# Gated linear attention and a rational MLP on one core: alpha loaded first, k turned in 112 columns, last products by token block, and GpSimd waits for VectorE operations on its port

## The chip, the cores and the metric

The kernel runs on one core of a Trainium2 chip. A core has five engines that work side by side, each through its own list of instructions in the order in which they were issued: TensorE (PE, matrix products), VectorE (DVE), ScalarE (ACT), GpSimd (POOL) and SyncE (SP, which here only issues transfers, or DMAs). An instruction waits on semaphores until what it needs is done, and what stands behind it on its engine waits too. The metric is the device time of one execution in microseconds (us), less is better. All times below are in us unless marked ns.

## The reference

Two stages. The first is gated linear attention over q, k, v, alpha of shape (4, 8, 768, 48): batch, head, token, width.

```
for t in range(S):
    state = alpha[:, :, t, :, None] * state + einsum('bhd,bhe->bhde', k[:, :, t], v[:, :, t])
    y[:, :, t] = einsum('bhd,bhde->bhe', q[:, :, t], state)
```

y becomes x, 3072 tokens by 384. The second stage is an MLP with 2048 hidden units and a rational activation:

```
h = x @ w_in
g = (a0 + a1*h + a2*h**2 + a3*h**3) / (1 + |b0|*|h| + |b1|*h**2 + 1e-6)
out = g @ w_out
```

w_in and w_out arrive as float64, everything else as float32.

## The kernel before

Attention is cut into 24 chunks g of 128 tokens, six for each batch, with the eight heads as four pairs side by side. For a chunk VectorE forms the running products of alpha from behind (L445) and from the front (L457), k and q are multiplied by them (L472, L475, on POOL or DVE), PE makes the scores (L489), ACT copies them out (L496), POOL masks them (L500), PE turns k (L507) for the state's update and ACT copies it out (L510), the state is decayed (L513), and PE makes the chunk's output (L531, once with the state, once with scores and v) and the update (L550), which DVE adds (L560). The first four chunks' inputs come in whole lines (L393) and are turned on PE (L410); the others come as 32-row pieces (L386) and are turned on DVE (L437, L442).

The weights arrive as 64-bit words (L240, L243) in sixteen pieces, each joined into float32 (ACT L252 and L264, DVE L260 and L280) and split into a high and a low part (ACT L295; DVE or POOL L300), so that three products of reduced width stand for one exact one. The MLP's blocks u = 0 to 9 use whole float32 words (L625, L638); the others, u = 10 to 95, use the parts (L652 in; L671 out). Each block's 128x512 tile of h goes through a chain: ACT L698 (|h|) and L701, POOL or ACT L705/L707 (q1), POOL L710 (qm), DVE L721, L725, ACT L728, L731, DVE L735, L738, L744 (g), and for wide blocks ACT L747 (high part gh) and POOL or DVE L751 (low part gl). For the last 512 tokens PE puts tokens into rows (L665), and DVE and ACT copy the four token blocks out (L691, L689) and SP and ACT store them (L695).

What is computed is a list of some 2700 steps, each with an engine, some with an alternative engine, and what it comes after. The order in which steps are issued, and which take their alternative, stands in a packed table (ORDER) that `Plan.run` (L45) reads; each engine keeps that order. A step's costs and due times do not act when a table is read. A step has a mark `lock` where it is a VectorE operation that shares an SBUF port with GpSimd; before the change the mark has no effect on what is issued.

Of the kernel before, what the change touches and what calls it, by code (L numbers as in the profile page):

```python
# [24 lines left out]
class Plan:  # L25
# [42 lines left out]
    '0d~B7VXm8jc35aFbHh9~gKSq@$FwvPY;OC=OtiyoT{Fo}#mS-b>{Of8JTUX^NIS(AG1KfcJZ5I#J@b!kY{G0&^UO@Q6-',
    '~HpZ3f%vILgkjGx4TrV;0(n=82hUN89Hn#Iy=oU}xh?Gse!cdF)s_2i0^pvuzVo*(|YZ?JKj?j<c`LI$OznHH$(Q+bZU',
    'kd1IE@Z|1i7Vyc>cX1yJ1cG>0jt=Skl$Nn^p%nG}~el&S)Q?uKyv~z6-^Vw{&n{BB1WmegfHlOWbw%FCSr`c*x*>`4--',  # L70
    'DcmLxj4Y=3*B$On?Gi+-EI%qzh;Luu*NPzfPbx+8}^48Xb#%b_H5{Xw!fK&3-Gt;WFkN>bJHHOJMB4(aK;WYhwVcA$Fw',
    '!Q%@KRv&c{2Zk2z{D*kg7velXAN3wzt%vKMV+hy{Z~^4oj%l3juY>_~ImMga?#?R`sd#h$PXcWmE~t5%?$xn?_>0PfnC',
# [1067 lines left out]
```

## Time and profile before

| what | us |
|---|---|
| three runs | 548.06, 546.98, 545.26 (median 546.98) |
| profiled execution | 545.37, its span 543.6 |
| PE busy | 523.7 (96%) |
| DVE busy | 483.4 (89%) |
| ACT busy | 439.5 (81%) |
| POOL busy | 404.0 (74%) |

The span runs from the first to the last event of the profiled execution; 1.77 us of its own time lie around it. Busy shares are means over stages with different limits: attention and the preparation of weights fill DVE in the first fifth, and the wide blocks fill PE after it. A bracket such as [1.66 <-DVE t L744] at the end of a timeline row says that the engine had been idle for 1.66 us and that the operation of DVE at L744 that wrote t released it. A row with x12 stands for twelve instructions in a run. A mean duration of a product is longer than the pitch of a run of them, since they are pipelined.

### The profile page before, as it was taken

The page shows a single profiled execution, that of the slowest core. Times are in us where ns is not written, and L with a number is a line of the kernel's source. Part 1 is how long each engine was busy: PE and PEld are TensorE (multiplying, and loading weights), DVE is VectorE, ACT ScalarE, POOL GpSimd, SP SyncE. Part 2 cuts the span into 40 slices and gives each one's busy share as a digit, 9 for nine tenths or more (in the row PEclk, how much of TensorE's full clock was granted, in tenths as well). Part 3 has the DMA queues.
Part 4 walks back from the last instruction along what each step waited for, and adds up shares of the span by engine and source line. Part 5 has one row for each costly group of instructions (what it writes and reads, how often), then busy time and mean ns, then how long its engine had stood idle before and what let it go on. Part 6 is the DMA issues. An engine that isn't in the chain of part 4 may idle for free.

```text
span 543.6 us, 11871 instructions
## 1 busy us (share of the span) xinstructions
PE 523.7 (96%) x4350; PEld 433.0 (80%) x4350; DVE 483.4 (89%) x717; ACT 439.5 (81%) x737; POOL 404.0 (74%) x377
## 2 busy tenths in 40 slices
PE   8889898999999999999999999999999999999994
PEld 8778687788788777878788887888788877889994
DVE  2989989999998899999999999998899797888872
ACT  3899798999997788768787778898877778779781
POOL 2567677899997798788578667877788675786772
PEclk9998899999999999999999999999999999999998
DMA  9959966654543535643455232442553410040001
GB/s 251 307 117 279 247 170 156 143 127 117 134 126 81 129 77 116 118 118 66 102 111 108 60 74 58 94 97 69 112 114 72 93 23 20 2 78 1 1 1 61
DMA packets 146174, 57.46 MB, mean 106 GB/s; under 512 B 133056, under 2 KB 138688, under 8 KB 146112
## 3 DMA queue, kind: packets, MB, share of 16 engines
q1 hardware_dynamic: 145824, 56.27, 44.4%
q8 instruction: 35, 0.57, 0.5%
q10 hardware_dynamic: 288, 0.39, 0.2%
q14 instruction: 27, 0.22, 0.1%
HBM read 47.98 MB, written 4.72 MB: 97 GB/s over the span
## 4 chain that ended last, share of the span: by engine, by line
PE 66%; DVE 9%; DMA 9%; SPq 9%; issue 2%; ACT 2%; POOL 1%; DVEq 0%; ACTq 0%
PE ps L652 27%; PE ps L671 22%; PE ps L665 6%; SPq L386 5%; PE ps L531 4%; DMA wo_words<-in_moe_w_out_dram 4%; PE ps L489 3%; DMA wi_words<-in_moe_w_in_dram 3%; SPq L240 2%; PE ps L638 2%; DMA raw_a<-in_alpha_dram 1%; DVE t L725 1%; DVE ps L738 1%; DVE t L721 1%; DVE t L744 1%
## 5 line engine op out<-in xcount | busy, mean ns | idle before, releaser
L652 PE MATMUL ps<-x,wi 128*128 128x512 f32 x774 | 209.6, 397 | 0.2 <-DVE t L744 0.2
L671 PE MATMUL ps<-gh_gl,wo 128*128 128x512 f32 x630 | 176.0, 400 | 0.4 <-ACT gh_gl L747 0.4
L652 PEld LDWEIGHTS ps<-x,wi 128*128 128x128 f32 x774 | 143.7, 188 | 33.1 <-DVE t L744 1.7
L710 POOL TENSOR_TENSOR qm<-qm,ah 128x512 f32<-128x512 f32 x96 | 127.3, 1326 | 30.2 <-ACT qm L707 21.6
L671 PEld LDWEIGHTS ps<-gh_gl,wo 128*128 128x128 f32 x630 | 115.4, 188 | 27.9 <-ACT gh_gl L747 0.8
L751 POOL TENSOR_TENSOR gh_gl<-t,gh_gl 128x512 fp32r<-128x512 f32 x76 | 98.9, 1302 | 33.3 <-ACT gh_gl L747 11.3
L701 ACT ACTIVATE t<-ps,coef 128x512 f32<-128x512 f32 x96 | 74.3, 774 | 15.8 <-PE ps L652 9.2
L698 ACT ACTIVATE ah<-ps 128x512 f32<-128x512 f32 x96 | 57.2, 596 | 34.0 <-PE ps L652 24.5
L735 DVE SCALAR_TENSOR_TENSOR t<-t,coef,ps 128x512 f32<-128x512 f32 x96 | 70.7, 738 | 15.1 <-ACT ps L731 14.5
L721 DVE TENSOR_TENSOR t<-t,ps 128x512 f32<-128x512 f32 x96 | 64.9, 676 | 14.6 <-ACT t L701 10.7
L728 ACT ACTIVATE ps<-qm,one_eps 128x512 f32<-128x512 f32 x96 | 66.3, 691 | 11.7 <-POOL qm L710 5.9
L725 DVE SCALAR_TENSOR_TENSOR t<-t,coef,ps 128x512 f32<-128x512 f32 x96 | 70.9, 740 | 2.0 <-ACT ah L698 0.7
L705 POOL TENSOR_SCALAR qm<-ah,bab 128x512 f32<-128x512 f32 x53 | 43.0, 811 | 37.2 <-ACT ah L698 28.7
L744 DVE SCALAR_TENSOR_TENSOR t<-ps,t 128x512 f32<-128x512 f32 x96 | 65.8, 686 | 1.9
L738 DVE SCALAR_TENSOR_TENSOR ps<-qm,ps 128x512 f32<-128x512 f32 x96 | 66.0, 687 | 0.0
L747 ACT ACTIVATE gh_gl<-t 128x512 fp32r<-128x512 f32 x86 | 53.9, 627 | 7.0 <-DVE t L744 6.7
L731 ACT ACTIVATE ps<-ps 128x512 f32<-128x512 f32 x96 | 56.0, 584 | 1.8
L665 PE MATMUL ps<-wo,gh_gl 128*128 128x384 f32 x192 | 38.0, 339 | 0.0
L445 DVE TENSOR_TENSOR_SCAN tg<-ta,ps 128x528 f32<-128x528 f32 x24 | 29.9, 1244 | 8.7 <-ACT ta L429 8.7
L472 POOL TENSOR_TENSOR tqk<-tqk,tg 128x512 f32<-128x512 f32 x22 | 29.5, 1340 | 10.2 <-ACT parts L252 9.0
L665 PEld LDWEIGHTS ps<-wo,gh_gl 128*128 128x128 f32 x192 | 34.4, 188 | 2.4 <-ACT gh_gl L747 0.3
L500 POOL TENSOR_SCALAR_AFFINE_SELECT sc<-sc 128x1024 f32<-128x1024 f32 x24 | 26.9, 1120 | 12.0 <-ACT sc L496 9.7
(114 smaller groups left out, 745.3 us busy)
## 6 DMA issues: line engine op xcount, KB each, us to landing
raw_qk<-in_q_dram SPq DMA_DIRECT2D x160, 48.0 KB, 2.1
raw_a<-in_alpha_dram SPq DMA_DIRECT2D x160, 48.0 KB, 2.1
raw_qk<-in_k_dram SPq DMA_DIRECT2D x160, 48.0 KB, 2.1
wi_words<-in_moe_w_in_dram SPq DMA_DIRECT2D x8, 768.0 KB, 7.9
wo_words<-in_moe_w_out_dram SPq DMA_DIRECT2D x8, 768.0 KB, 7.0
tv<-in_v_dram SPq DMA_DIRECT2D x24, 192.0 KB, 3.2
wr<-in_alpha_dram SPq DMA_DIRECT2D x18, 256.0 KB, 3.0
out_dram<-parts SPq DMA_DIRECT2D x60, 64.0 KB, 2.1
```

What stands on the lines that cost most here:

```text
L652: nc.tensor.matmul(h_of(u), w(key)[:, kt * FU + f % FU, :], x[:, kt, xp, :], start=(n == 0), stop=(n == len(todo) - 1),)
L665: nc.tensor.matmul(bank(T_BANKS[tt], DM), g[:, tt * P : (tt + 1) * P], w(("o", f // FU))[:, f % FU, :], start=(f == 0 and first_w), stop=( ...
L671: nc.tensor.matmul(bank(O_BANKS[dt]), w(("o", f // FU))[:, f % FU, dt * P : (dt + 1) * P], g, start=(f == 0 and first_w), stop=(f == NF - ...
L701: nc.scalar.activation(buf(s, "t1", u), h_of(u), AF.Identity, bias=a2, scale=a3)
L710: nc.gpsimd.tensor_tensor(buf(s, "qm", u), buf(s, "qm", u), buf(s, "ah", u), op=ALU.mult)
L721: nc.vector.tensor_tensor(t, t, h_of(u), op=ALU.mult)
L725: nc.vector.scalar_tensor_tensor(t, t, a1, h_of(u), op0=ALU.add, op1=ALU.mult)
L728: nc.scalar.activation(h_of(u), buf(s, "qm", u), AF.Abs_reciprocal_sqrt, bias=one_eps)
L735: nc.vector.scalar_tensor_tensor(t, t, a0, h_of(u), op0=ALU.add, op1=ALU.mult)
L738: nc.vector.scalar_tensor_tensor(h_of(u), buf(s, "qm", u), 1.0 + 1e-6, h_of(u), op0=ALU.add, op1=ALU.mult)
L744: nc.vector.scalar_tensor_tensor(t, h_of(u), 2.0, t, op0=ALU.subtract, op1=ALU.mult, reverse0=True)
L751: eng.tensor_tensor(buf(s, "gl", u).rearrange("p a b -> p (a b)"), buf(s, "t1", u), gh, op=ALU.subtract)
```

## The change

Six edits. Numbers after L are lines of the kernel before. (1) The first three loads on SP's queue are alpha, k, q; before, q, alpha, k. (2) PE's first instructions, transposes of the identity that write to nothing used (L403), number 20; before, 28. ACT gets a first instruction "prime" on a 128x1 tile, and the memset of one_eps that it reads stands earlier on POOL. (3) k is turned in 112 columns: a pair of heads fills 64 + 48 rows, and the last 16 of 128 held nothing needed; the copy after it has 448 columns in place of 512, and 16 columns of the tile get zeros once. (4) The twelve products of the last block, u = 95, go by token block, through `last_out`. (5) For each VectorE step with the mark `lock`, the next POOL step in the issued order gets a wait for it; the step "tot" gets the mark when it is on DVE. (6) The table is new, as the steps' numbers are, but the order on each engine is otherwise kept; constants of the planner (SV, WIDE, kb and the like) change and are not read.

The diff, without the table's rows but the first of each and without numbers that only the planner reads:

```diff
@@ -42,102 +42,112 @@
-    def run(self, engines):
+    def run(self, engines, tc):
...
+        info = mybir.DependencyInfo(mybir.DependencyClass.Sync, mybir.DependencyReason.DATA)
+        held = None
         for n in order:
             key = keys[n & 0x7FFF]
             s = self.steps[key]
             assert all(a in done or a not in self.steps for a in s["after"])
+            mode = s["alt"] if key in self.other else s
+            old = len(tc.nc.cur_bb.bb.instructions)
             if s["alt"]:
-                s["fn"](engines[(s["alt"] if key in self.other else s)["eng"]], *s["args"])
+                s["fn"](engines[mode["eng"]], *s["args"])
             else:
                 s["fn"](*s["args"])
+            new = tc.nc.cur_bb.bb.instructions[old:]
+            if mode["lock"]:
+                held = new[-1]
+            elif mode["eng"] == "POOL" and held is not None:
+                tc.add_manual_dep(new[0], held.name, info, reason="shared port")
+                held = None
             done.add(key)
 
 
 ORDER = [
-    'c-jTQ17KK55CG7f*}?9wZQHhO+qUg%+7wA`+qUj%+qP}Hz4s;>W1JahA{cMbOfln4U?!N9CYqUQrkluSfr(+Fn`tJBiD',
...
+    'c-jrtV}mBV4gk<5O_R23+qP}nwr%^}XJ&S^wr$(CZQHhS?=LuCk5c2*6g5#9#mcFu$}3dkRTMQrrBkuhR5e}2PzzLC6-',
...
 ]
...
-WARM = 28
+WARM = 20
...
+    first_act = const.tile([P, 1], F32, name="first_act")
...
-    kts = ring("kt", NSC, [P, NC4, P])
+    KW = P - GAP
+    kts = ring("kt", NSC, [P, NC4 * KW + GAP])
...
     def set_st():
         nc.gpsimd.memset(st_d, 0.0)
+        nc.gpsimd.memset(kts[0][:, NC4 * KW :], 0.0)
...
     def k_turn(g):
         for a in range(NPAIR):
-            nc.tensor.transpose(bank(SCB)[:, a * P : (a + 1) * P], tk[g % NQ][:, a, :], ident)
+            nc.tensor.transpose(bank(SCB)[:, a * KW : (a + 1) * KW], tk[g % NQ][0:KW, a, :], ident[0:KW, 0:KW])
 
     def k_evac(g):
-        nc.scalar.activation(kts[g % NSC].rearrange("p a c -> p (a c)"), bank(SCB), AF.Copy)
+        nc.scalar.activation(kts[g % NSC][:, 0 : NC4 * KW], bank(SCB, NC4 * KW), AF.Copy)
...
                         nc.tensor.matmul(
-                            kv_bank()[r : r + 32, a * D : (a + 1) * D], kt[:, a, r : r + 32],
+                            kv_bank()[r : r + 32, a * D : (a + 1) * D], kt[:, a * KW + r : a * KW + r + 32],
...
+    def last_out(u, tt, gx):
+        f = jobs[u][2]
+        g = buf(fast_bufs, gx, u).rearrange("p a b -> p (a b)")
+        for w in (hi, lo) if gx == "gh" else (hi,):
+            nc.tensor.matmul(
+                bank(T_BANKS[tt], DM), g[:, tt * P : (tt + 1) * P], w(("o", f // FU))[:, f % FU, :],
+                start=False, stop=gx == "gl",
             )
...
+    add("prime", "ACT", 1.5, nc.scalar.activation, (first_act, one_eps, AF.Copy), ["one_eps"])
...
-            add(("tot", g), "POOL", 0.24, totals, (g,), [("suf", g), "halves", "consts", ("d", g - NQ)], alt=("DVE", 0.15, False))
...
+            add(("tot", g), "POOL", 0.24, totals, (g,), [("suf", g), "halves", "consts", ("d", g - NQ)], alt=("DVE", 0.16, True))
...
+            if u == NUA - 1:
+                for tt in range(PER):
+                    prev = [("ol", u - 1), ("og", tt - 1)]
+                    old = [("ws", m - 1, dt) for dt in range(KT)]
+                    add(("og", tt), "PE", 0.35, last_out, (u, tt, "gh"), [("gh", u), ("lo", ("o", j))] + prev, due=at)
+                    add(("ot", tt), "PE", 0.175, last_out, (u, tt, "gl"), [("og", tt), ("ot", tt - 1), ("gl", u)], lat=0.13, due=at + 2)
+                    add(("wd", m, tt), "ACT" if tt % 2 else "DVE", 0.5, last_done, (nc.scalar if tt % 2 else nc.vector, tt), [("ot", tt)] + old, due=at + 3)
+                    add(("ws", m, tt), "ACT" if tt % 2 else "SP", DMA, last_store, (nc.scalar if tt % 2 else nc.sync, tt), [("wd", m, tt)], kb=0.55)
+                continue
...
-            if f == NF - 1 and m == NSUP - 1:
-                for tt in range(PER):
...
-    plan.run({"DVE": nc.vector, "POOL": nc.gpsimd, "ACT": nc.scalar})
+    plan.run({"SP": nc.sync, "DVE": nc.vector, "POOL": nc.gpsimd, "ACT": nc.scalar}, tc)
```

On SP, at the program's start (raw_a, raw_qk and raw_second are the tiles for alpha, for k with q, and for the second 512 tokens; L393 is load_nat), before:

```order
L393 DMA raw_qk_80<-in_q_dram 128x8x96
L393 DMA raw_a_79<-in_alpha_dram 128x8x96
L393 DMA raw_qk_80<-in_k_dram 128x8x96
L240 DMA wi_words<-in_moe_w_in_dram 128x3x512
L393 DMA raw_second<-in_alpha_dram 128x8x96
L393 DMA raw_second<-in_k_dram 128x8x96
```

and in the changed kernel, where load_nat is L406 and the weights' load L251:

```order
L406 DMA raw_a_80<-in_alpha_dram 128x8x96
L406 DMA raw_qk_81<-in_k_dram 128x8x96
L406 DMA raw_qk_81<-in_q_dram 128x8x96
L251 DMA wi_words<-in_moe_w_in_dram 128x3x512
L406 DMA raw_second<-in_alpha_dram 128x8x96
L406 DMA raw_second<-in_k_dram 128x8x96
```

q's load moves from the first place to the third; the rest of the queue has its order.

On POOL, around the mask of chunk 4 (qm is the denominator's tile, L705 and L710 its two steps; sc the scores, L500 their mask; tqk k and q, L475 the multiplication of q; wo and wi the weights' parts, L300), before:

```order
L705 TENSOR_SCALAR qm_108<-ah_103,bab 128x512 [waits DVE_49,Activation_49]
L710 TENSOR_TENSOR qm_108<-qm_108,ah_103 128x512 [waits Pool_49]
L500 AFFINE_SELECT sc_99<-sc_99 128x1024 [waits Activation_49]
L475 TENSOR_TENSOR tqk_89<-tqk_89,fp_84 128x512
L300 TENSOR_TENSOR wo_950<-wr_77,wo_950 128x2x384 [waits DMAHW7_49,Activation_49]
L300 TENSOR_TENSOR wi_958<-wr_76,wi_958 128x6x128 [waits DMAHW0_49,Activation_49]
```

and in the changed kernel (L727, L732, L513, L488, L311):

```order
L727 TENSOR_SCALAR qm_109<-ah_104,bab 128x512 [waits DVE_49,Activation_49]
L732 TENSOR_TENSOR qm_109<-qm_109,ah_104 128x512 [waits DVE_49,Pool_49]
L513 AFFINE_SELECT sc_100<-sc_100 128x1024 [waits DVE_49]
L488 TENSOR_TENSOR tqk_90<-tqk_90,fp_85 128x512
L311 TENSOR_TENSOR wo_945<-wr_78,wo_945 128x2x384 [waits DMAHW7_49,Activation_49]
L311 TENSOR_TENSOR wi_953<-wr_77,wi_953 128x6x128 [waits DMAHW0_49,Activation_49]
```

The order is the same. The second and the third row now wait for DVE: the second for a step on the weights' words (L260), the third, the mask, for the joining of a weight (L280, the last of three in a run, at 85.91 in the trace of before).

On PE, the last block's products (gh_gl is the high and low part of g, wo_1518 and wo_1513 the last piece of w_out), before:

```order
L665 MATMUL ps<-wo_1518,gh_gl 128x384 [waits Activation_49]
L665 MATMUL ps<-wo_1518,gh_gl 128x384 x7
L665 MATMUL ps<-wo_1518,gh_gl 128x384 [waits Pool_49]
L665 MATMUL ps<-wo_1518,gh_gl 128x384 x3
L810 MATMUL ps<-ones,tot_beyond 1x1 [waits DVE_49]
```

and in the changed kernel (L693 is last_out):

```order
L693 MATMUL ps<-wo_1513,gh_gl 128x384 [waits Activation_49]
L693 MATMUL ps<-wo_1513,gh_gl 128x384 x5
L693 MATMUL ps<-wo_1513,gh_gl 128x384 [waits Pool_49]
L693 MATMUL ps<-wo_1513,gh_gl 128x384 x5
L832 MATMUL ps<-ones,tot_beyond 1x1 [waits DVE_49]
```

Before, eight products with the high part precede four with the low part. In the changed kernel six with the high part stand ahead of the wait for POOL's low part; behind it the blocks are finished one by one, the fourth block's two high products in between.

## Rows read from the trace of the kernel before

**Rows 1.** Stretch, length, busy of PE, PEld, DVE, ACT, POOL (count), clock, DMA share, GB/s.
```profile
96.00:536.00 440.00, 438.19 (x3467) 357.82 (x3465) 401.75 (x603) 362.19 (x631) 344.30 (x297) 1.00 0.37 81
```

**Rows 2.** The same for PE alone, four stretches.
```profile
20.00:96.00 76.00, 68.69 (x757) 0.96 0.80 205
40.00:45.00 5.00, 4.81 (x93) 0.66 1.03 345
180.00:200.00 20.00, 18.99 (x171) 1.00 0.44 103
240.00:280.00 40.00, 39.21 (x351) 1.00 0.45 97
```

**Rows 3.** Chain of waits, 82 to 90: start, length, what.
```profile
82.02 0.95 DVE tqk L442
...
83.19 1.93 DVE wr L280
...
89.29 0.69 DVE t L744
```

**Rows 4.** Timeline, start: start, length, instruction, idle before it and what ended that.
```profile
1.43 0.57 SPq L393 DMA_DIRECT2D raw_a<-in_alpha_dram  x1
...
1.51 6.09 PE L403 MATMUL ps<-ident 128*128 128x128 f32 x28 [1.51 <-POOL ident masks.py:199]
...
9.43 1.28 ACT L429 ACT_TABLE_LOAD   x1 [9.43 <-PE ps L410]
...
11.36 1.25 DVE L445 TENSOR_TENSOR_SCAN tg<-ta,ps 128x528 f32<-128x528 f32 x1 [8.65 <-ACT ta L429]
```

**Rows 5.** Timeline at 39 to 41: the first wait that is for transfers.
```profile
39.05 1.25 DVE L442 STREAM_TRANSPOSE tqk<-raw_qk 128x1024 f32<-128x1024 f32 x1 [1.23 <-DMA raw_qk<-in_q_dram]
...
39.96 0.86 PE L531 MATMUL ps<-tqk,st_d 128*32 128x128 f32 x24 [1.72 <-ACT kt L510]
```

**Rows 6.** The transposes of k: one turn on the timeline, and all of them.
```profile
36.30 0.60 PE L507 MATMUL ps<-ident,tqk 128*128 128x128 f32 x4
...
L507 PE MATMUL ps<-ident,tqk 128*128 128x128 f32 x80 | 12.1, 274 | 0.8 <-ACT sc L496 0.7
```

**Rows 7.** VectorE lines: count, shortest/median/longest ns, first and last start.
```profile
L260 DVE TENSOR_SCALAR wo_words<-wo_words x8: 530/721/1434, 26.3 to 98.3; 128x768 uint32<-128x768 uint32 x8
...
L751 DVE TENSOR_TENSOR gh_gl<-t,gh_gl x10: 666/686/1635, 115.2 to 498.3; 128x512 fp32r<-128x512 f32 x10
```

**Rows 8.** Timeline at 255 to 260.
```profile
255.52 1.29 POOL L710 TENSOR_TENSOR qm<-qm,ah 128x512 f32<-128x512 f32 x1
...
255.73 1.64 DVE L751 TENSOR_TENSOR gh_gl<-t,gh_gl 128x512 fp32r<-128x512 f32 x1
...
259.41 1.43 PE L652 MATMUL ps<-x,wi 128*128 128x512 f32 x5 [0.24 <-DVE t L744]
```

**Rows 9.** Timeline at 82 to 90.
```profile
81.96 1.11 POOL L500 TENSOR_SCALAR_AFFINE_SELECT sc<-sc 128x1024 f32<-128x1024 f32 x1
...
85.05 0.94 DVE L280 SCALAR_TENSOR_TENSOR parts<-parts,wi_words 128x768 uint32<-128x768 uint32 x1
...
86.97 1.06 PE L531 MATMUL ps<-sc,tv 128*32 128x128 f32 x32
...
90.03 2.21 PE L625 MATMUL ps<-x_whole,wi_words 128*128 128x256 f32 x9 [1.66 <-DVE t L744]
```

**Rows 10.** Busy time of POOL alone, columns as in rows 2.
```profile
100.00:160.00 60.00, 56.42 (x42) 1.00 0.49 124
```

**Rows 11.** Timeline, the end.
```profile
527.67 8.47 PE L665 MATMUL ps<-wo,gh_gl 128*128 128x384 f32 x46
...
533.71 1.29 POOL L751 TENSOR_TENSOR gh_gl<-t,gh_gl 128x512 fp32r<-128x512 f32 x1 [0.75 <-ACT gh_gl L747]
...
536.18 0.49 ACT L689 ACTIVATE parts<-ps 128x384 f32<-128x384 f32 x1 [2.60 <-PE ps L665]
...
537.78 0.34 ACTq L695 DMA_DIRECT2D out_dram<-parts  x1
```

More of the change, by code (lines that the diff above doesn't have):

```diff
@@ L68 @@
[L68 to L72, printed above, removed]
@@ L129 @@
 DMA = 0.49
-SV = (1.1, 2.03, 0.67, 0.46)
+SV = (0.9, 1.95, 0.68, 0.4)
 IN = (1.09, 1.31)
 OH = (0.722, 1.3)
-WIDE = 0.232
+WIDE = 0.234
 G3 = 4
@@ L943, in tile_gla_then_rational_mlp @@
                 + [("join" if kept(x) else "lo", x) for i, x in enumerate(keys) if wr_slot(i) == b % WB]
-                + [("lo", x) for x in brings[:b][-WB:][:1] if b >= WB], kb=1.5)
+                + [("lo", x) for x in brings[:b][-WB:][:1] if b >= WB], kb=1.35)
             add(("hi", key), "ACT", 0.85, split_hi, (key, b % WB), [("bring", key)] + [("in" if key[0] == "i" else "oh", u, 1) for u in user[-1:]])
@@ L960, in tile_gla_then_rational_mlp @@
                 add(("tn", m, nm, par), "PE", 0.9, turn_nat, (m, nm, par),
-                    [("nat", m, nm), "ident", "warm"] + before + ([("nat", m, "k"), ("set", "k", m)] if nm == "q" else []), lat=0.13)
+                    [("nat", m, nm), ("set", nm, m), "ident", "warm"] + before + ([("nat", m, "k"), ("set", "k", m)] if nm == "q" else []), lat=0.13)
     for g in range(NGC):
@@ L976, in tile_gla_then_rational_mlp @@
                     ov = [("tn", 0, x, p) for p in range(2) for x in ("a" if nm == "a" else "kq")]
[L977 removed]
+                    add(("ld", nm, g, qd), "SP", 2 * DMA, load_akq, (nm, g, qd), [("ta" if nm == "a" else "tqk", g - 1), ("set", nm, 0)] + ov, kb=0.23)
         if m >= NNAT:
@@ L997, in tile_gla_then_rational_mlp @@
         if not last(g):
-            add(("kt", g), "PE", 0.42, k_turn, (g,), [("se", g), ("k", g)], lat=0.13)
-            add(("ke", g), "ACT", 0.6, k_evac, (g,), [("kt", g), ("am", g - NSC)])
+            add(("kt", g), "PE", 0.38, k_turn, (g,), [("se", g), ("k", g)], lat=0.13)
+            add(("ke", g), "ACT", 0.55, k_evac, (g,), [("kt", g), ("am", g - NSC), "set_st"])
         if not first(g):
@@ L1074, in tile_gla_then_rational_mlp @@
                     add(("ws", m, dt), "SP", 4 * DMA, wide_store, (m, dt), [("wd", m, dt)], kb=1.8)
-            if f == NF - 1 and m == NSUP - 1:
-                for tt in range(PER):
-                    old = [("ws", m - 1, dt) for dt in range(KT)]
-                    add(("wd", m, tt), "ACT" if tt % 2 else "DVE", 0.5, last_done, (nc.scalar if tt % 2 else nc.vector, tt), [("ol", u)] + old, due=at + 3)
-                    add(("ws", m, tt), "ACT" if tt % 2 else "SP", DMA, last_store, (nc.scalar if tt % 2 else nc.sync, tt), [("wd", m, tt)], kb=0.7)
             continue
@@ L1099, in tile_gla_then_rational_mlp @@
     add("vd_mm", "PE", 0.3, verdict_mm, (), ["vd_sum", "vd_ones", ("xl", 2 * NBLK - 1), ("xh", 2 * NBLK - 1)], lat=0.13)
-    add("vd_ok", "DVE", 0.15, verdict_ok, (), ["vd_mm"], lat=5.0)
+    add("vd_ok", "DVE", 0.15, verdict_ok, (), ["vd_mm"], lat=1.0)
     ENG = mybir.EngineType
```

131 lines of the change are left out of this document (68 added, 63 removed).

## The prediction

> **What bounds the kernel now.** I read the stretches of busy time first, then PE's idle brackets on the timeline, then the chain of waits. From 96 to 536 PE is busy for 438.19 of 440 us at full clock [rows 1], so nothing in the middle of the program can gain more than the 1.81 us that PE idles there, unless PE's own work gets less. The idle time is in two stretches: 1.01 us in 180 to 200 and 0.79 in 240 to 280 [rows 2]. Ahead of that PE is busy for 68.69 of 76 us in 20 to 96, so 7.3 us stand idle, and one stretch there, 40 to 45, ran at a mean clock of 0.66 [rows 2], that is, partly at 1.2 GHz in place of 2.4. The chain of waits says what holds PE in that part: at 82.02 DVE's transpose of k and q, then a VectorE operation of 1.93 us on the weights (L280), then DVE without a gap to the g of a block at 89.29 [rows 3], which PE awaited for 1.66 us at 90.03 [rows 9]. So there are three sorts of time to win: PE's own instructions, PE's idle time ahead of 96 and at two places behind, and the end. A saving anywhere else is swallowed by the next wait.
>
> **Alpha first, 20 warming transposes, prime.** The 28 transposes take 6.09 us, 0.2175 each [rows 4]; eight fewer end 1.74 earlier, alpha's load moves up one place, and the 1.28 of ACT's table load, which stands between the first turned tile and its copy, goes to where ACT is idle for 9.43 us [rows 4]. DVE's first scan, which idles for 8.65 us and begins at 11.36 [rows 4], can so begin about 2 to 2.5 us earlier (less than 1.74 + 1.28 = 3.0, because alpha must land too). But at 39.05 DVE idles for 1.23 us until a transfer lands, and PE behind it for 1.72 [rows 5]: whatever was ahead by then waits for the queue, whose landings no compute step of the start holds up. I take 0 for the end of the program; the bounds are -2.0 (all of it carried to the end) and 0. Only q comes later, by two places, and it is needed after the second scan.
>
> **112 columns.** Four transposes take 0.60, one alone 0.274, so the pitch is (0.60 - 0.274)/3 = 0.109 [rows 6]. An eighth of it, 16 of 128 columns, is 0.0137; for 80 transposes 1.1 us. The 20 turns are spread evenly over the program, and those ahead of 90 lie beside waits, so about three quarters count: -0.8. No row shows whether a narrower transpose is shorter in proportion, so the bounds are 0 and -1.1. The copy after it gets an eighth shorter too, on ACT, which PE does not wait for behind 96; I count nothing.
>
> **The waits on GpSimd.** Both engines are slower when they meet. L260 takes 0.53 us at its shortest and 1.434 at its longest, L751 on DVE 0.666 and 1.635 [rows 7]; at 255.73 the long L751 begins 0.21 after POOL's qm began and ends 0.56 after it does [rows 8]. With the waits POOL stands aside in such a pair, and DVE runs at its short time. What that is worth is read at the places where PE waits.
> At 82 to 90, the L280 of 1.93 us [rows 3] ran beside POOL; the next of the same size took 0.94 [rows 9]. It stands on the chain to PE's 1.66 us, so -1.0.
> At 255 to 259, the L751 of 1.64 would take its median of 0.686, and DVE's next steps lead to PE's wait at 259.41 [rows 8]. The saving is 0.95, but PE idles only 0.79 in that stretch [rows 2], so -0.8.
> At 180 to 200 I can name no stretched operation on the way to PE's 1.01 us of idle time; half of it, -0.5, is a choice between 0 and -1.0.
> Elsewhere after 96 there is no idle time to win, and ahead of 82 the next wait is for a transfer. Together -2.3; the most is 1.66 + 1.01 + 0.79 = 3.5.
> The price: behind each waiting POOL instruction stands all that POOL has to do. The dearest is the mask of chunk 4. It ran at 81.96 and will now wait for the third L280 in the run, which began at about 85.9 and takes some 0.95, and ends 1.0 earlier than now: about 85.9. So the mask comes 3.9 us later and ends at about 87.0. Its user, PE's product on the scores, began at 86.97 [rows 9], which just holds. POOL's multiplication of q, two low parts of weights and the next qm stand behind it. POOL idles for 3.58 of 60 us in 100 to 160 [rows 10], so it catches up slowly; this I price as a rival, below, and as +0 here.
> The Trainium skill, "SBUF — State Buffer", section "Who interferes with whom", says of the port pair that DVE and GpSimd share that whoever issues first holds it for the whole instruction and the other fully blocks, and that issue order decides who blocks. Rows 8 agree: when the long L751 began, POOL's qm had 1.08 left, and 1.08 and its own 0.686 are 1.77, near the 1.64 that it took. That rule speaks against the edit: a wait in place of a blocked port only names the loser beforehand. By it alone the -2.3 would be near 0.
>
> **The clock.** PE's wait at 90.03 turns into one some 3 us earlier, when the mask ends. Gaps at 38 to 40 were followed by a stretch at a mean clock of 0.66, which costs up to 0.34 x 5 = 1.7 us [rows 2, 5]; the gap at 90.03 was not, as far as the row from 96 shows [rows 1]. Bounds 0 and +1.7; I take +0.5.
>
> **The last block.** The low part is ready at 533.71 + 1.29 = 535.00, and the products have a pitch of 8.47/46 = 0.184 [rows 11]. Six high products end by 535.0 too. Then block 0 is done at about 535.25, block 1 at 535.43, and ACT's first copy can begin at about 535.55, where it began at 536.18; ACT's copy, store, copy, store then take the same 1.60 to the issue of the last store at 537.78 [rows 11]. So -0.6, with 0 and -0.7 as bounds: the fourth block's two high products lie in the shadow of ACT's copy and store.
>
> **Sum.** 0 - 0.8 - 2.3 + 0.5 - 0.6 = -3.2. On the profiled execution of 545.37 (a span of 543.6 and 1.77 around it) that is 542.2. This execution was 1.6 below the median of the three runs; the four times that are known have a mean of 546.4, and from that level the sum gives **543.2**. Its own range runs from -5.3 (every saving at its bound, no clock term) to about -0.5: 541.1 to 546.
>
> **Rivals.**
> A. The ports are a zero sum. POOL loses by waiting what DVE wins, and hands it on by qm and the masks; left are the columns and the end: 546.4 - 1.4 = 545.0. For it: POOL is busy for 56.42 of 60 us in 100 to 160 [rows 10], so a wait put on it is not free there. Against it: at 82 and at 255 DVE, and not POOL, was on the way to PE [rows 3, 8]. Chance 0.24.
> B. Slower: POOL's backlog reaches PE. The place is the mask of chunk 4, the price the 3.9 us by which it moves. It decides if the mask ends after 87, or if the low parts and the qm behind it come after ACT is ready for them: then PE's products on the scores, and the blocks' g, are late by most of it, and with 3.58 us of slack in 60 [rows 10] POOL cannot make it good before the 1.81 us of PE's later idle time are gone. The saving of the ports is lost then: 546.4 - 1.4 + 0.5 + 3.9 = 549.4. Against it: the estimate of 87.0 for the mask, and POOL was idle just before and after in 80 to 90, having run ahead. Chance 0.15.
> C. The start's 2 us are carried to the end, because the queue of transfers itself begins to move earlier: 543.2 - 2.0 = 541.2. For it: 8.65 us of idle DVE [rows 4]. Against it: the wait for a transfer at 39.05 [rows 5] and again the one behind 82.02. Chance 0.08.
> The sum above has the remaining 0.53.
>
> **How the numbers follow.** About 0.5%, or 2.7 us, is what a measurement of this kernel can tell from no change; against the median of 546.98 faster begins below 544.2. Of the forecast's 0.53 some 0.37 lie there, of A's 0.24 some 0.06, and all of C: 0.51. The same: 0.15 of the forecast, 0.17 of A, 0.03 of B, 0.35 in all. Slower: 0.12 of B and 0.02 of the others, 0.14. The range of 8 in 10 takes in A, C's middle and the lower half of B: 540.6 to 548.2.
>
> **What would show it.** In the changed kernel's profile DVE's L260, L280 and L751 have no long ones left, and DVE's busy time falls, while POOL's waits name DVE. The first scan begins near 9; the wait for a transfer at 39 is still there, longer. The mask of chunk 4 begins near 86, and PE's idle time in 82 to 92 is about 1 us less than now. The turns take about 0.55. The last store is issued near 537.15 less what was won ahead. I am wrong if DVE's long ones are gone and PE's idle time is as large as before (A), if PE idles more behind 86 with POOL as what it waited for (B), or if DVE's step at 39.05 comes 2 us earlier (C).

## The result, and the profile after

Four runs of the changed kernel took 538.35 to 540.07 us, median 539.28; four runs of the kernel before on the same chip had a median of 547.52. The ratio is 0.9868 with an interval of 0.9842 to 0.9894, that is, 7.2 us less (5.8 to 8.7); the two medians differ by 8.2. The prediction had 3.2 less and a lower end of 540.6: the direction was right, the size less than half. The two profiled executions, 545.37 and 539.54, differ by 5.8.

The page of the changed kernel, its busy times and its chain of waits by engine (before, PE held 66% of that chain and DVE 9%):

```profile
PE 520.4 (97%) x4342; PEld 429.2 (80%) x4342; DVE 478.3 (89%) x717; ACT 439.4 (82%) x738; POOL 393.5 (73%) x378
...
PE 80%; DMA 7%; SPq 4%; DVE 3%; ACT 3%; issue 2%; POOL 1%; ACTq 0%; DVEq 0%; POOLq 0%
```

DVE's busy time fell by 5.1 us and POOL's by 10.5. That both fell says that neither simply handed its time to the other. Not all of DVE's long operations are gone, as the prediction's sign wanted: L271 still takes up to 0.88, L291 1.34 and L773 1.01. PE's fell by 3.3, of which eight transposes of the start are 1.74.

In the changed kernel's lines, L271 answers to L260 (words), L291 to L280, L458 to L445 (first scan), L455 to L442 (turn of k and q), L513 to L500 (mask), L544 to L531, L747 to L725, L766 to L744 (g), L773 to L751 (low part), L693 to L665 and L717 to L695 (last products, last stores). Its timeline at the places of [rows 3, 4, 5, 8, 9] (start, length, instruction, idle before it and what ended that):

```profile
9.10 1.25 DVE L458 TENSOR_TENSOR_SCAN tg<-ta,ps 128x528 f32<-128x528 f32 x1 [6.36 <-ACT ta L442]
...
38.30 0.86 PE L544 MATMUL ps<-tqk,st_d 128*32 128x128 f32 x24 [2.04 <-ACT kt L523]
...
38.80 1.25 DVE L455 STREAM_TRANSPOSE tqk<-raw_qk 128x1024 f32<-128x1024 f32 x1 [2.96 <-DMA raw_qk<-in_q_dram]
...
80.59 1.25 DVE L455 STREAM_TRANSPOSE tqk<-raw_qk 128x1024 f32<-128x1024 f32 x1 [2.98 <-DMA raw_a<-in_alpha_dram]
81.76 0.92 DVE L291 SCALAR_TENSOR_TENSOR wr<-wr,wo_words 128x768 uint32<-128x768 uint32 x1
...
83.47 0.95 DVE L291 SCALAR_TENSOR_TENSOR wr<-wr,wi_words 128x768 uint32<-128x768 uint32 x1
...
84.49 1.09 POOL L513 TENSOR_SCALAR_AFFINE_SELECT sc<-sc 128x1024 f32<-128x1024 f32 x1 [5.45 <-DVE wr L291]
...
85.64 1.93 PE L544 MATMUL ps<-sc,tv 128*32 128x128 f32 x32 [2.42 <-POOL sc L513]
...
86.85 0.68 DVE L766 SCALAR_TENSOR_TENSOR t<-ps,t 128x512 f32<-128x512 f32 x1
...
253.36 0.69 DVE L773 TENSOR_TENSOR gh_gl<-t,gh_gl 128x512 fp32r<-128x512 f32 x1
...
255.35 0.69 DVE L766 SCALAR_TENSOR_TENSOR t<-ps,t 128x512 f32<-128x512 f32 x1
```

Read against before, these starts tell where this profile gained. The first scan is 2.26 earlier (11.36), the turn at 39.05 only 0.25: that is the transfer's wait, now 2.96 long, as forecast. The turn of chunk 6 is 1.43 earlier (82.02 in rows 3), which the forecast had at nothing. The L291 after it takes 0.92 in place of 1.93, so that the g at 89.29 is 2.44 earlier: that 1.0 had been forecast. The low part at 255.73 is 2.37 earlier, and 0.69 long in place of 1.64; the g after it, at 258.66 before, is 3.31 earlier. The mask of chunk 4 began at 84.49, not near 86, because the whole place had moved up; PE waited 2.42 for it. PE's idle time in 82 to 92 is therefore 2.42 and not 1.0 less than the 1.66 of before, and PE's next block begins 1.89 earlier (88.14 in place of 90.03), 0.46 beyond what the turn had moved.

One profile does not fix such starts. Kernels whose instructions are the same up to there differ in them: in before and the five kernels below that differ from it only behind 527, the turns of 64.23 and 82.02 begin at 64.04 to 64.73 and at 80.74 to 82.03; in a_early and a_nomask4 the turn of 38.80 begins at 36.91 and 38.93, and in a_early that of 80.59 at 78.27. Starts ahead of 100 are thus known to about 2 us. Behind 170 two steps are the same within 0.02 in each of the six kernels that were compared and have the later waits: 0.62 between 170 and 177 and 0.94 between 251 and 259. What an edit is worth is taken from the timed runs.

PE in stretches of the changed kernel (stretch, length, busy, granted clock, DMA share, GB/s):

```profile
86.00:88.00 2.00, 2.00 (x64) 0.50 1.04 326
...
180.00:200.00 20.00, 19.33 (x173) 1.00 0.38 87
240.00:280.00 40.00, 39.91 (x355) 1.00 0.47 101
```

The idle time in 240 to 280 went from 0.79 to 0.09, in 180 to 200 from 1.01 to 0.67 [rows 2]. Behind the gap that ends at 85.64 PE ran at 1.2 GHz (0.50 in 86 to 88); before it did so for part of 40 to 45 [rows 2] and of 60 to 65 (0.69), and these two stretches are at full clock here.

The end of the changed kernel, which answers to [rows 11]:

```profile
530.09 1.30 POOL L773 TENSOR_TENSOR gh_gl<-t,gh_gl 128x512 fp32r<-128x512 f32 x1 [0.74 <-POOL gh_gl L773]
530.21 2.54 PE L693 MATMUL ps<-wo,gh_gl 128*128 128x384 f32 x12
...
532.51 1.04 SPq L717 DMA_DIRECT2D out_dram<-parts  x2
...
533.09 0.14 DVE L835 TENSOR_SCALAR ok<-ps 1x1 int32<-1x1 f32 x1
...
533.70 0.34 ACTq L717 DMA_DIRECT2D out_dram<-parts  x1
```

From the end of the low part (531.39) to the last store's issue 2.31 pass; before it was 535.00 to 537.78, 2.78. That is 0.47 less, near the forecast 0.6. But from that issue to the end of the span 4.0 pass (533.70 to 537.7), and before 5.8 (537.78 to 543.6). For this 1.8 the prediction had no term.

So three things stand against the forecast: time won ahead of 82, time won behind the last issue, and whether each edit did it. The experiments take the edits one at a time, each timed in five rounds against the kernel before.

### The profile page after: what moved, and what is told of

It is laid out like the page before. It is cut to its first block, busy times and chain, and to the rows that moved or that the text cites. A ratio compares the mean times of both kernels' runs of the same rounds, so it can differ in the third digit from the quotient of the medians.

```text
span 537.7 us, 11876 instructions
## 1 busy us (share of the span) xinstructions
PE 520.4 (97%) x4342; PEld 429.2 (80%) x4342; DVE 478.3 (89%) x717; ACT 439.4 (82%) x738; POOL 393.5 (73%) x378
## 3 DMA queue, kind: packets, MB, share of 16 engines
HBM read 47.98 MB, written 4.72 MB: 98 GB/s over the span
## 4 chain that ended last, share of the span: by engine, by line
PE 80%; DMA 7%; SPq 4%; DVE 3%; ACT 3%; issue 2%; POOL 1%; ACTq 0%; DVEq 0%; POOLq 0%
PE ps L665 32%; PE ps L684 26%; DMA wo_words<-in_moe_w_out_dram 6%; PE ps L678 6%; PE ps L544 6%; PE ps L502 3%; SPq L399 3%; PE ps L651 2%; PE ps L520 1%; PE ps L563 1%; PE ps L423 1%; PE ps L416 1%; PE ps L638 1%; ACT sc L509 1%; DMA raw_qk<-in_q_dram 1%
## 5 line engine op out<-in xcount | busy, mean ns | idle before, releaser
L665 PE MATMUL ps<-x,wi 128*128 128x512 f32 x774 | 209.4, 397 | 0.0
L665 PEld LDWEIGHTS ps<-x,wi 128*128 128x128 f32 x774 | 143.8, 188 | 32.4 <-DVE t L766 0.4
L732 POOL TENSOR_TENSOR qm<-qm,ah 128x512 f32<-128x512 f32 x96 | 124.3, 1295 | 23.9 <-ACT qm L729 11.8
L773 POOL TENSOR_TENSOR gh_gl<-t,gh_gl 128x512 fp32r<-128x512 f32 x76 | 98.8, 1300 | 32.6 <-PE ps L684 11.4
L747 DVE SCALAR_TENSOR_TENSOR t<-t,coef,ps 128x512 f32<-128x512 f32 x96 | 71.0, 740 | 2.0 <-ACT ah L720 0.7
L727 POOL TENSOR_SCALAR qm<-ah,bab 128x512 f32<-128x512 f32 x53 | 41.1, 776 | 36.5 <-ACT ah L720 17.5
L766 DVE SCALAR_TENSOR_TENSOR t<-ps,t 128x512 f32<-128x512 f32 x96 | 65.8, 686 | 1.9
L513 POOL TENSOR_SCALAR_AFFINE_SELECT sc<-sc 128x1024 f32<-128x1024 f32 x24 | 26.3, 1096 | 21.8 <-DVE wr L291 5.5
L485 POOL TENSOR_TENSOR tqk<-tqk,tg 128x512 f32<-128x512 f32 x22 | 28.4, 1293 | 12.4 <-DVE ta L467 7.2
L458 DVE TENSOR_TENSOR_SCAN tg<-ta,ps 128x528 f32<-128x528 f32 x24 | 29.9, 1244 | 6.4 <-ACT ta L442 6.4
L678 PE MATMUL ps<-wo,gh_gl 128*128 128x384 f32 x180 | 35.4, 336 | 0.0
L729 ACT ACTIVATE qm<-ah,bab 128x512 f32<-128x512 f32 x43 | 34.9, 814 | 0.3
```

The lines of the kernel that those rows point to most:

```text
L665: nc.tensor.matmul(h_of(u), w(key)[:, kt * FU + f % FU, :], x[:, kt, xp, :], start=(n == 0), stop=(n == len(todo) - 1),)
L678: nc.tensor.matmul(bank(T_BANKS[tt], DM), g[:, tt * P : (tt + 1) * P], w(("o", f // FU))[:, f % FU, :], start=(f == 0 and first_w), stop=( ...
L732: nc.gpsimd.tensor_tensor(buf(s, "qm", u), buf(s, "qm", u), buf(s, "ah", u), op=ALU.mult)
L747: nc.vector.scalar_tensor_tensor(t, t, a1, h_of(u), op0=ALU.add, op1=ALU.mult)
L766: nc.vector.scalar_tensor_tensor(t, h_of(u), 2.0, t, op0=ALU.subtract, op1=ALU.mult, reverse0=True)
L773: eng.tensor_tensor(buf(s, "gl", u).rearrange("p a b -> p (a b)"), buf(s, "t1", u), gh, op=ALU.subtract)
```

## Experiments

**One edit alone, and all but one.** b_waits puts the waits alone into the kernel before; a_nowaits takes them from the changed one.

```diff
 # b_waits, in Plan.run of before (and "tot" gets the mark)
+            if mode["lock"]:
+                held = new[-1]
+            elif mode["eng"] == "POOL" and held is not None:
+                tc.add_manual_dep(new[0], held.name, info, reason="shared port")
+                held = None
 # a_nowaits, in Plan.run of the changed kernel
-                tc.add_manual_dep(new[0], held.name, info, reason="shared port")
```

> The kernel before with GpSimd's fifty waits alone. Ports ahead of 90 (the waits save VectorE time on the joined weights at 53 to 58, where I counted nothing): 542 to 544, 3 to 5 below the kernel before, and no half-clock stretch at 60 to 65. Start (the 2 us won at the start are what is carried): 545 to 546, 1.5 to 2 below, as the prediction's own term of -2.3 + 0.5.

> The changed kernel without GpSimd's waits. Ports: 3 to 5 above the changed kernel (542.5 to 544.5), with long VectorE operations back and PE idle near 59 to 61. Start: at most 2 above it (541).

Measured: b_waits 0.9912 (0.9893 to 0.9931), 4.8 us less; a_nowaits 542.88, 0.9929 (0.9909 to 0.995). Its ratio is 0.0061 above that of the changed kernel, or 3.3 us, known to about 1.8. The waits are the largest part, at 3.3 to 4.8 and not 2.3, and the ports are no zero sum. In a_nowaits DVE is busy for 484.4 and POOL for 403.6, with the waits for 478.3 and 393.5.

b_start has the start's edits alone, a_oldstart the changed kernel without them.

```diff
 # b_start, in before
-WARM = 28
+WARM = 20
+            order[n] = keys.index(("nat", 0, "akq"[i]))
+        nc.scalar.activation(first_act, one_eps, AF.Copy)
 # a_oldstart, in the changed kernel
+            order[n] = keys.index(("nat", 0, "qak"[i]))
-WARM = 20
+WARM = 28
-    add("prime", "ACT", 1.5, nc.scalar.activation, (first_act, one_eps, AF.Copy), ["one_eps"])
+    add("prime", "ACT", 1.5, lambda: None, (), ["one_eps"])
```

> The kernel before with the start alone: alpha, k, q; 20 transposes; the table load early. Ports: within 1 us of the kernel before, the 2 us being lost at the wait for a transfer near 39. Start: 2 to 4 below the kernel before.

> The changed kernel with the start as before: q, alpha, k; 28 transposes; no early instruction on ACT. Ports: within 1 us of the changed kernel. Start: 2 to 4 above it.

Measured: b_start 0.9986 (0.9972 to 1.0); a_oldstart 0.9845 (0.9818 to 0.9872), not slower than the changed kernel. Alone the start is worth 0.8 us (0 to 1.5), at the edge of the noise; beside the other edits nothing can be seen of it.

b_112 has the narrow turns alone, b_tail the last block's order alone.

```diff
 # b_112
-            nc.tensor.transpose(bank(SCB)[:, a * P : (a + 1) * P], tk[g % NQ][:, a, :], ident)
+            nc.tensor.transpose(bank(SCB)[:, a * KW : (a + 1) * KW], tk[g % NQ][0:KW, a, :], ident[0:KW, 0:KW])
 # b_tail
+    def last_out(u, tt, gx):
...
-            add(("ol", u), "PE", WIDE * KT, wide_out, (u, hi, "gl"), ...
+            add(("ol", u), "PE", WIDE * KT, last_rest if end else wide_out, ...
```

> The kernel before with k turned in 112 columns, nothing else. If the columns' shorter transposes are what counts: -0.8 (545.5), evenly over the program. If the narrower copy or another phase of the clock counts more: -2 to -3 (543 to 544), with the gain in one place ahead of 96.

> The kernel before with the last block's products by token block alone. If only the issue of the last store counts: -0.6 (545.7). If the spacing of the four stores makes them land sooner as well, as the 1.8 us between the last store's issue and the end of the changed kernel say: -2 to -2.5 (544).

Measured: b_112 1.0 (0.9986 to 1.0014), b_tail 0.9957 (0.9944 to 0.997), 2.3 us less. A turn in b_112 on the timeline, beside the 0.60 of [rows 6]:

```profile
36.29 0.55 PE L509 MATMUL ps<-ident,tqk 112*128 112x112 f32 x4
```

The turn is as short as forecast, and the time does not move. The four parts measured alone add up to 4.8 + 2.3 + 0.8 + 0 = 7.9, near the 7.2 of the whole; within the noise (some 1.7 on the sum) none takes from another.

**Which waits.** There are 50, 23 of them ahead of 90. a_early keeps the first 23 in the changed kernel, b_late puts only the other 27 into the kernel before.

```diff
 # a_early
+                pair += 1
+                if pair <= 23:
+                    tc.add_manual_dep(new[0], held.name, info, reason="shared port")
 # b_late
+                if pair > 23:
+                    tc.add_manual_dep(new[0], held.name, info, reason="shared port")
```

> The changed kernel with the first 23 of the 50 waits, those ahead of 90. If the gain is made ahead of 90: 541 less nothing, 1 to 1.5 above the changed kernel. If it is made at 255, as the prediction had it for 0.8 of 2.3: 2 above it.

> The kernel before with the last 27 of the fifty waits, those behind 90. The prediction's terms for 180 to 200 and 255 to 259: -0.5 and -0.8, so 1.3 below the kernel before, in steps at 174 to 190 and at 255. If later idle time of PE takes it back: within 0.4.

Measured: a_early 0.989 (0.9871 to 0.9909), b_late 0.9978 (0.9968 to 0.9987), 1.2 less where 1.3 had been forecast for the later places. So the early waits are worth about 3.6 on the kernel before (4.8 less 1.2) and 2.1 in the changed one (0.9929 less 0.989), known to about 1.2 and 1.5; 1.0 had been forecast. The later gain at 170 to 177 is that of one short operation, DVE's step tot, which ran beside POOL's mask. In before, then in b_late, with the low part at 255:

```profile
172.48 0.95 DVE L463 TENSOR_TENSOR tot<-tg,halves 128x8 f32<-128x8 f32 x1
```

```profile
172.30 0.35 DVE L475 TENSOR_TENSOR tot<-tg,halves 128x8 f32<-128x8 f32 x1
...
254.91 0.69 DVE L763 TENSOR_TENSOR gh_gl<-t,gh_gl 128x512 fp32r<-128x512 f32 x1
...
256.90 0.69 DVE L756 SCALAR_TENSOR_TENSOR t<-ps,t 128x512 f32<-128x512 f32 x1
```

Against 255.73 and 258.66 of before, 0.82 is won ahead of the low part (0.63 of it between 170 and 177) and 0.94 more by it.

Where a part of the early gain is won shows on the timeline of DVE and POOL at 53 to 58. Before:

```profile
53.50 1.09 POOL L500 TENSOR_SCALAR_AFFINE_SELECT sc<-sc 128x1024 f32<-128x1024 f32 x1
...
53.57 1.43 DVE L260 TENSOR_SCALAR wo_words<-wo_words 128x768 uint32<-128x768 uint32 x1
...
54.93 2.02 DVE L280 SCALAR_TENSOR_TENSOR wo_words<-wr,wo_words 128x768 uint32<-128x768 uint32 x1
...
56.11 2.92 POOL L254 TENSOR_SCALAR parts<-wi_words 128x768 f32<-128x768 f32 x1
...
56.87 1.27 DVE L260 TENSOR_SCALAR wi_words<-wi_words 128x768 uint32<-128x768 uint32 x1
...
58.06 0.73 DVE L735 SCALAR_TENSOR_TENSOR t<-t,coef,ps 128x512 f32<-128x512 f32 x1
```

and in b_waits (L270, L290 and L745 are L260, L280 and L735; L510 the mask, L264 is L254):

```profile
53.48 0.61 DVE L270 TENSOR_SCALAR wo_words<-wo_words 128x768 uint32<-128x768 uint32 x1
54.01 0.95 DVE L290 SCALAR_TENSOR_TENSOR wo_words<-wr,wo_words 128x768 uint32<-128x768 uint32 x1
54.88 0.55 DVE L270 TENSOR_SCALAR wi_words<-wi_words 128x768 uint32<-128x768 uint32 x1
55.35 1.40 DVE L745 SCALAR_TENSOR_TENSOR t<-t,coef,ps 128x512 f32<-128x512 f32 x2
...
55.57 1.09 POOL L510 TENSOR_SCALAR_AFFINE_SELECT sc<-sc 128x1024 f32<-128x1024 f32 x1 [1.89 <-DVE wi_words L270]
...
57.90 2.21 POOL L264 TENSOR_SCALAR parts<-wi_words 128x768 f32<-128x768 f32 x1
```

Three operations in a row take 4.72 - 2.11 = 2.6 us less when POOL stands aside, by one wait: that of the mask of chunk 3. POOL pays 2.07 for its mask and gets 0.71 back on L264. b_sm3 has this wait alone, b_nosm3 the other 22 early ones.

```diff
 # b_sm3
+                if key == ("sm", 3):
+                    tc.add_manual_dep(new[0], held.name, info, reason="shared port")
 # b_nosm3
+                if pair <= 23 and key != ("sm", 3):
+                    tc.add_manual_dep(new[0], held.name, info, reason="shared port")
```

> The kernel before with one of the fifty waits: chunk 3's mask (POOL L500 at 53.5) for the third of three VectorE steps on weights. If the early gain is made there (three stretched VectorE steps at 53 to 58 cost 2.6 us, and VectorE's turn of chunk 4 starts the loads whose landing is awaited at 82): VectorE's turn at 64 comes 2 us earlier, the one at 82 1.5 to 2 earlier, and the time is 1.5 to 3 below the kernel before. If the gain is spread over the early waits, or a transfer at 82 swallows it: within 0.7 of the kernel before.

> The kernel before with the other 22 of the first 23 waits. If the gain is made at chunk 3's mask: 0.5 to 1.5 below the kernel before, by the join at 83. If it is spread: 2.5 to 3.5 below.

Measured: b_sm3 0.9965 (0.995 to 0.998), 1.9 less by one wait among fifty; b_nosm3 0.9949 (0.9927 to 0.9971), 2.8 less (1.6 to 4.0). In b_sm3 the three operations take 0.56, 0.95 and 0.56, in b_nosm3 0.62, 1.84 and 1.63. So the one wait shortens them and is worth about 1.9; but the other 22 give more than the 0.5 to 1.5 that was expected if the gain were made here, so the early gain is not at this one place, and where else it is made, beyond the joined weight at 82, was not found. In b_sm3's profile the turn of 64.23 begins at 62.58, outside the scatter given above, that of 82.02 at 80.66, inside it, and the gain stays about 2.1 to the end.

**Why the transfers' wait did not swallow it.** The turn of k and q reads raw_qk, of which there is one buffer: the next loads wait for it (the turns of 39.05, 64.23 and 82.02 are those of chunks 4, 5 and 6; an expectation above calls the second that of chunk 4). SP's queue in 40 to 84 of before shows one such wait, beside longer ones for other transfers (engine, line, what it waited for: total, times, longest):

```profile
SPq L386 <- DMA wi_words<-in_moe_w_in_dram: 6.4, 2, 4.0
...
SPq L386 <- DVE tqk L442: 1.4, 1, 1.4
```

And the two turns of k and q there, in before:

```profile
64.23 1.23 DVE L442 STREAM_TRANSPOSE tqk<-raw_qk 128x1024 f32<-128x1024 f32 x1
...
82.02 1.25 DVE L442 STREAM_TRANSPOSE tqk<-raw_qk 128x1024 f32<-128x1024 f32 x1 [1.15 <-DMA raw_qk<-in_q_dram]
```

and in b_waits:

```profile
62.31 1.25 DVE L452 STREAM_TRANSPOSE tqk<-raw_qk 128x1024 f32<-128x1024 f32 x1 [1.05 <-DMA wi_words<-in_moe_w_in_dram]
...
80.29 1.25 DVE L452 STREAM_TRANSPOSE tqk<-raw_qk 128x1024 f32<-128x1024 f32 x1 [2.88 <-DMA raw_a<-in_alpha_dram]
```

At 64.23 before, DVE did not wait at all: it was DVE that was late. DVE alone in 42 to 64 of before (stretch, length, busy, granted clock, DMA share, GB/s) idles for 0.52 of 22 us:

```profile
42.00:64.00 22.00, 21.48 (x31) 0.89 0.96 259
```

From one turn to the next 16.5 to 19.6 us pass in the profiles of all runs (17.8 in before, 18.0 in b_waits, 17.3 in b_112, b_tail and a_nowaits, 18.1 in b_sm3, 18.5 in the changed kernel). In b_sm3, b_waits and the changed kernel the first turn comes 1.7 to 2.1 earlier than in before and the second 1.4 to 1.7: in these profiles the wait at 82 took back a little and not all. A reading that fits is that a gain at 53 moves the turn at 64, the loads after it and the wait at 82. That the queue follows the turn is not shown: most of its waiting there is for the weights' transfers, and no second buffer was tried.

**The price of a wait.** a_nomask4 leaves out of the changed kernel the one wait that the slower rival hung on, and a_best leaves out both it and the new start.

```diff
 # a_nomask4 (a_best: this, and a_oldstart's edit)
+                if key != ("sm", 4):
+                    tc.add_manual_dep(new[0], held.name, info, reason="shared port")
```

> The changed kernel without one of the fifty waits, the one of chunk 4's mask for the last of three joins of weights. If the wait costs PE's gap of 2.4 near 85 and a half-clock stretch behind it: 1 to 2.5 below the changed kernel (537 to 538). If the join's longer time beside the mask takes it back: the same, within 0.5.

> The changed kernel with the start as before and without the wait of chunk 4's mask. If both are small gains that add: 536.5 to 538, 1.5 to 2.5 below the changed kernel. If they are noise: 538 to 540.

Measured: a_nomask4 0.9862 (0.9843 to 0.988), a_best 0.988 (0.9853 to 0.9906). Neither can be told from the changed kernel (to about 1.7 us), and no version tried beats it clear of the noise. That does not price PE's 2.42 at nothing: without this wait the mask runs at 77.58, and PE idles nearly as long for the next thing, DVE's g:

```profile
85.68 2.86 PE L639 MATMUL ps<-x_whole,wi_words 128*128 128x256 f32 x12 [2.29 <-DVE t L767]
```

Counted from the turn of chunk 6, PE's next block begins 6.99 behind it there (85.68 - 78.69) and 7.55 in the changed kernel (88.14 - 80.59), so at that place the wait costs about 0.6. PE's clock in a_nomask4 (columns as above):

```profile
40.00:45.00 5.00, 4.19 (x71) 0.66 1.05 341
...
86.00:88.00 2.00, 2.00 (x11) 1.00 0.99 183
```

Its instructions up to that mask are those of the changed kernel, whose 40 to 45 ran at 1.00. So a half-clock stretch at that place comes and goes from one profile to the next.

**What follows the last issue.** Two guesses on b_tail's 1.8 us (540.7 - 536.66 in place of 543.6 - 537.78) behind the issue were tried on the kernel before: that the first two stores go out at the same moment (b_split and b_split3 cut one copy of ACT in two), and that they go over two queues (b_oneq puts all four on SP's).

```diff
 # b_split (tt == 1), b_split3 (tt == 3)
-            eng.activation(o, bank(T_BANKS[tt], DM), AF.Copy)
+            for c in (slice(0, 352), slice(352, DM)) if tt == 3 else (slice(0, DM),):
+                eng.activation(o[:, c], bank(T_BANKS[tt], DM)[:, c], AF.Copy)
 # b_oneq
-        eng.dma_start(out[r : r + P, :], parts[:, tt * DM : (tt + 1) * DM])
+        nc.sync.dma_start(out[r : r + P, :], parts[:, tt * DM : (tt + 1) * DM])
```

> The kernel before with ACT's first copy of the last block cut in two (352 and 32 columns), so that ACT's first store starts some 0.2 later than SP's first store instead of at the same moment. If stores that start together are what lands late: the end comes 4.0 behind the last store's issue in place of 5.8, and the time is 1.3 to 1.8 below the kernel before. If the gap of 0.39 between SP's two stores is what lands late: 5.8 again, and the time 0.2 above.

> The kernel before with ACT's first copy of the last block cut in two (352 and 32 columns), now the copy that comes first, so that ACT's first store starts some 0.2 behind SP's first. If stores that start together land late: the end comes 4.0 behind the last store's issue in place of 5.8, and the time is 1.3 to 1.8 below the kernel before. If it is something else, as the 0.39 between SP's two stores: 5.8, and the time 0 to 0.2 above.

> The kernel before with all four last stores issued by SP. If two queues whose stores are interleaved land late: the last issue comes 0.2 later, the end 4.0 behind it, and the time is 1.3 to 1.8 below the kernel before. If not: 0.2 above it.

Measured: 0.9999 (0.9983 to 1.0016), 1.0003 (0.9992 to 1.0014) and 0.9987 (0.9976 to 0.9998). b_split cut the wrong copy (the first stores stayed 0.01 apart) and says nothing; b_split3 moved them only 0.06 apart, still 5.8 to the end; b_oneq, whose four stores are issued some 0.45 apart on one queue, has 5.5. Neither two queues nor stores at the same moment are the cause.

What differs is in the profile of the transfers. Before, two stretches at the end (queue, kind: packets, MB, share; then median us to landing), the first of 539.3 to 540.8, the second of 534 to 544:

```profile
q14 instruction: 4, 0.03, 6.4%
q8 instruction: 1, 0.02, 4.0%
...
out_dram<-parts SPq DMA_DIRECT2D x2, 192.0 KB, 3.4
```

The changed kernel, 535.5 to 536.4 and 530 to 538:

```profile
q14 instruction: 4, 0.03, 10.8%
q8 instruction: 1, 0.02, 8.9%
...
out_dram<-parts SPq DMA_DIRECT2D x2, 192.0 KB, 2.1
```

Five packets that the profile calls instruction, 8 to 16 KB each, move once near the end, 2.2 to 2.8 us after the verdict that the program writes last on DVE (L835 at 533.09 in the changed kernel). In before the verdict stands here:

```profile
536.58 0.13 DVE L813 TENSOR_SCALAR ok<-ps 1x1 int32<-1x1 f32 x1
```

Of the 16 parts of the last store, before, 13 have landed by 540.19 and three at 541.87 to 542.00; in b_oneq four are late. That these are the parts that share a transfer engine with the packets fits, but the profile does not name the engine. Before, the packets start at 539.41 to 540.11, amid the stores, which run from 537.55 to 541.52; after, at 535.58 to 536.05, as the stores (533.36 to 535.64) end. In b_tail they start at 538.54 and the stores end at 538.60. The new order brings the packets out of the stores' way: the last store is issued 0.61 behind the verdict in place of 1.20, and the stores now end as the packets begin. b_latevd tests it: before, with three operations on DVE that do nothing needed ahead of the verdict.

```diff
 # b_latevd
+        for _ in range(3):
+            nc.vector.memset(bank(0), 0.0)
```

> The kernel before with three clearings of a finished PSUM bank (0.48 each by the one at the start) on VectorE ahead of the verdict L813, so that the verdict and the five instruction packets that follow it by 2.8 come 1.4 later; products, copies and stores as before. If these packets of 8 and 16 KB, which run from 539.4 among the stores' last ones, are what lands the stores late: the stores land at about 540 in place of 542.0 (by the profile, from the last store's issue 2.3 in place of 4.2) and the time is 1 to 1.8 below the kernel before. If the stores land late for another reason: 4.2 again, and the time 0 to 1 above.

Measured: 0.9964 (0.9951 to 0.9977), 2.0 less (1.3 to 2.7), by adding work. The profiled execution is the slowest of its five (545.39, the others 543.97 to 544.20) and was already 1.4 behind the profile of before at 137, so the way from the issue on is what to read in it. Its timeline and then its transfers in 541.9 to 542.9 and 534 to 544:

```profile
539.16 0.34 ACTq L695 DMA_DIRECT2D out_dram<-parts  x1
...
539.88 0.14 DVE L815 TENSOR_SCALAR ok<-ps 1x1 int32<-1x1 f32 x1
```

```profile
q14 instruction: 4, 0.03, 9.8%
q8 instruction: 1, 0.02, 5.9%
...
out_dram<-parts SPq DMA_DIRECT2D x2, 192.0 KB, 2.4
```

The stores land 2.45 after the last issue in place of 4.2, and the packets come after them, from 542.06; the span ends 4.5 after the issue in place of 5.8.

## Why the prediction was right and wrong

| term | forecast | measured alone |
|---|---|---|
| start | 0 | -0.8 (-1.5 to 0) |
| 112 columns | -0.8 | 0 (-0.8 to +0.8) |
| waits, at 180 and 255 | -1.3 | -1.2 (-1.7 to -0.7) |
| waits, ahead of 96 | -1.0 | -3.6 (4.8 less 1.2); -2.1 in the changed kernel |
| clock | +0.5 | not separate |
| last block | -0.6 | -2.3 (-3.1 to -1.6) |

**The step that failed first** is the sentence that ahead of 82 "the next wait is for a transfer". It put the whole early part on the one place at 82 and all else ahead of it at nothing. At 82 the join came out 1.0 shorter, as worked out, though PE, which now waits for the mask, got only 0.46 of it. Ahead of it one wait on GpSimd alone, at 53 to 58, was worth 1.9 to the end (b_sm3), and the early waits together 2.1 to 3.6. In 42 to 64 DVE is busy for 21.48 of 22 us and does not wait for a transfer at 64.23, so time that it loses there is lost; the transfer's wait at 82.02 moved with it and took back only a part. Why it moved is read, not shown: through the single buffer the loads follow DVE's previous turn. The rows to see it were there: the long L260 and L280 at 53.57 to 56.87, and the SP queue's wait for tqk. For the start the same reasoning held: its 2.26 at the first scan shrank to 0.25 at 39.05 in this profile, and the timed runs give 0 to 1.5. A reading beside it was wrong: the prediction has PE at 39.96 wait behind that turn, but the row names ACT's copy of k, and in the changed kernel this product begins 1.66 earlier (38.30) with a turn 0.25 earlier.

**The step that failed second** is the last block's: its sum ended at the issue of the last store, and left the way from issue to landing as it was. The part up to the issue was right (-0.47 against -0.6). The rest, -1.8, is stores that land sooner. b_latevd shows that what follows DVE's verdict had held them up; the instruction packets are the only other transfers that the profile shows there.

**112 columns** were mis-sized: the turn became 0.05 shorter, as worked out, and 20 of these were not seen in the time (b_112: 0, -0.8 to +0.8). Nor do they add up on its timeline: the g of the block at 163 comes 0.11 earlier than before, that of 491 0.15 later. Why PE's shorter turns do not shorten the run, though PE is all but always busy behind 96, is not settled; 0.8 is also the edge of what the interval excludes.

**The later waits** came out as forecast in sum. At 255 it is the long low part, shown in b_late. At 180 half the idle time had been taken with no operation named, which was a guess; 0.35 of its 1.01 went, and starts behind it moved by 0.6, by the tot at 172.48.

**The range.** Its lower side of -5.3 adds up the bounds of the columns, the waits and the end and leaves out the -2.0 that the start had been given; with it the sum is -7.3. But the start gave little of what was missing.

**The clock.** Behind the gap for the mask came the half-clock stretch that was priced, in this profile, and the two of before were missing in it. Over all runs of a kernel the mean granted clock is 0.9923 for before, 0.9923 for b_waits and 0.9938 for the changed kernel, so the clock does not carry the difference. It goes with part of the scatter: of the 104 runs of before that were timed beside the experiments, ten at 0.987 have a mean of 547.7, eight at 0.995 one of 545.4. Why stretches come and go stays open.

**The rivals.** A (a zero sum of the ports) fell with a_nowaits and b_waits, and with both engines' busy times. The Trainium skill, "SBUF — State Buffer", section "Who interferes with whom", says that issue order decides which of the two blocks. The runs agree in so far as a change of who goes first moves the loss, and here it was worth 0.9912. They differ from the picture of one engine that holds the ports and another that pays: at 56.87 before, L260 began behind POOL's L254, ended ahead of it and took 1.27 in place of 0.55, and L254 took 2.92 in place of 2.21, so in this profile both lost. B (POOL's backlog) showed its sign in part, PE waiting for POOL at 85.64, but not its price: the run was faster, and a_nomask4 gains nothing by leaving that wait out. C (the start carried to the end) fell with b_start and a_oldstart.

## What to carry to other kernels

A wait for a transfer need not swallow a gain ahead of it: look up what the load waited for, and if one of its waits is for a single buffer's last reader on the engine that gains, do not put the gain at nothing. A sum for the end of a kernel goes to the last landing, not to the last issue, and what else is in the transfer queues there counts. Where two engines slow each other, both may lose; let the one step aside whose lateness reaches nobody, and look for the places where the other is never idle.
